# Casting the filter early on GpSimd, and making the swapped stage-P weights there too

## The chip, the cores and the metric

The kernel runs on one core of a Trainium2 chip. The metric is the device time of one execution in microseconds (us). Times are medians of several executions. All the runs used here are fast (a single core's runs are sorted only by how far they lie above the fastest of the same kernel), and the granted clock is named where it matters. Engines: TensorE (PE in the profile), VectorE (DVE), ScalarE (ACT), GpSimd (POOL), and SyncE (SP), which issues nearly all transfers.

## The reference

Eight sequences of 3008 x 256 are filtered in the frequency domain, then every token goes through a squared-ReLU feed-forward layer:

```python
X = np.fft.rfft(x, axis=1)                        # x: 8 x 3008 x 256, float32
Y = X * (filt_r + 1j * filt_i)[None, :, :]        # filters: 1505 x 256
y = np.fft.irfft(Y, n=3008, axis=1)
h = np.maximum(y.reshape(24064, 256) @ w_in, 0.0)   # w_in 256 x 2048
out = (h * h) @ w_out                               # w_out 2048 x 256
```

## The kernel before

The transform is split into stages. Stage A multiplies x by a small DFT matrix and writes u to memory (dU). u is read back transposed, stage B transforms it, VectorE multiplies by the filter F (the "products"), stage P transforms back, ScalarE evicts that as ze, and ze goes to memory (dZ). The z reads bring it back, and stage Y finishes y. Batch 0 goes through all this in a prologue. Batches 1 to 7 are woven into the feed-forward "stream", which takes over at the end of the prologue.

F has to be brought into the layout of stage B: the filter is cast to half precision (`f16`), then permutation matmuls "place" it into PSUM, from which it is evicted into `sF`. Stage P needs its weights twice for batch 0, once with the two halves of the partitions swapped (`sSPx`). The parts that matter here, with cuts marked:

```python
p_ze = tc.tile_pool(name="p_ze", bufs=3)    # ze: three groups of stage P in flight
p_h2 = tc.tile_pool(name="p_h2", bufs=2)    # two 16 KB buffers, used in turn
# ... third x tile of batch 0 (from p_h2), filters f32s[0], f32s[1] loaded on SyncE ...
u0 = p_h2.tile([96, NM, D], F16, tag="h2", name="u0")
for k, eng in enumerate((nc.vector, nc.vector, nc.gpsimd)):    # casts of batch 0's x
    ...
for c in (0, 2, 1, 3):
    chunk_a(0, c)            # stage A into u0
    write_u(0, c)            # u0 -> dU
# ... loads: half of sSB and sSP, u, the other halves, w_in, x(1,0), x(1,1) ...
f16s.append(p_h2.tile([128, 2, QF + D], F16, tag="h2", name="f16"))
for i in range(2):
    nc.gpsimd.tensor_copy(out=f16s[0][:, i, QF:], in_=nyq[:, i, :])
for im, eng in enumerate((nc.gpsimd, nc.vector)):
    for e in (slice(0, 1504), slice(1504, QF)):
        eng.tensor_copy(out=f16s[0][:, im, e], in_=f32s[im][:, e])
    for k in range(6):
        place_f(im, k)
for k, eng in enumerate((nc.vector, nc.gpsimd)):
    ...                      # sSPx, two copies of 64 x 1536 each
cast_win()                   # GpSimd
for c in range(2):
    cast_x(1, c, nc.gpsimd)
for r in range(14):
    if r < 12: unit_b(0, r)          # stage B and product
    if r >= 2: unit_p(0, r - 2)      # stage P, ze; a dZ write after every third
for c in range(4): read_z(0, c)
load_wout()
# ... x(1,2), x(1,3), stage A of batch 1, 12 warming matmuls, stage Y, stream ...
```

Of the kernel before, what the change touches and what calls it, by code (L numbers as in the profile page):

```python
# [9 lines left out]
F16 = mybir.dt.float16  # L10
# [9 lines left out]
QF = 3008  # L20
# [84 lines left out]
def kernel(  # L105
# [9 lines left out]
    nc = tc.nc  # L115
    B, S, D = x.shape
# [25 lines left out]
    p_h2 = ctx.enter_context(tc.tile_pool(name="p_h2", bufs=2))  # L142
# [63 lines left out]
    for k, v in enumerate((v0[:, 0:8, :], v1, v0[:, 8:16, :])):  # L206
        t = (p_h2 if k == 2 else p_x32).tile([128, 8, D], F32, tag="h2" if k == 2 else "x32",
                                             name=f"x0_{k}")
# [4 lines left out]
    f32s = []  # L213
# [10 lines left out]
    nyq = p_out.tile([128, 2, D], F32, tag="ost", name="nyq")  # L224
# [4 lines left out]
    sSP = const.tile([128, NC, 128], F16, name="sSP")  # L229
# [18 lines left out]
    f16s = []  # L248

    def place_f(im, k):  # L250

        banks, groups = bank_pair(f"psf_{im}_{k}")
        for i in range(4):
            c = 4 * k + i
            e0, e1 = D * c, D * (47 - c)
            cuts = [0] + [d for d in range(1, D)
                          if (e0 + d) % QF == 0 or (c and (e1 + d) % QF == 0)] + [D]
            for d0, d1 in zip(cuts, cuts[1:]):
                o = banks[i // 2][:, (i % 2) * D + d0:(i % 2) * D + d1]
                q, a = divmod(e0 + d0, QF)  # L260
                nc.tensor.matmul(o, sPF[:, PQ.index((0, q)), :], f16s[0][:, im, a:a + d1 - d0],  # L261
                                 start=True, stop=False)
                q, a = divmod(e1 + d0, QF) if c else (0, QF + d0)
                nc.tensor.matmul(o, sPF[:, PQ.index((1, q)), :], f16s[0][:, im, a:a + d1 - d0],  # L264
                                 start=False, stop=True)
        eng = pair_engine()
        for t, i in groups:
            n = t.shape[1]
            dst = sF[:, im, 4 * k + 2 * i:4 * k + 2 * i + 2 * n, :]
            src = t.rearrange("p t (a d) -> p (t a) d", d=D)  # L270
            if eng is nc.scalar:
                eng.activation(out=dst, in_=src, func=AF.Copy, scale=sign[:, 0:1] if im else 1.0)
            elif im:
                eng.tensor_scalar_mul(out=dst, in0=src, scalar1=sign[:, 0:1])
            else:
                eng.tensor_copy(out=dst, in_=src)
# [30 lines left out]
    def write_u(b, c):  # L307
        nc.sync.dma_start(
            out=dU[b].rearrange("(m q) d -> q m d", q=96)[:, 8 * c:8 * c + 8, :],
            in_=us.pop((b, c)))  # L310
# [18 lines left out]
    def chunk_a(b, c):  # L329

        if b == 0:
            u = u0[:, 8 * c:8 * c + 8, :]
        else:
            u = p_u.tile([96, 8, D], F16, tag="u", name=f"u_{b}_{c}")
        us[(b, c)] = u
        for k in range(2):
            banks, groups = bank_pair(f"psA_{b}_{c}_{k}")
            for i in range(2):
                m = slice(4 * k + 2 * i, 4 * k + 2 * i + 2)
                o = banks[i][0:96]  # L340
                if b == 0:
                    nc.tensor.matmul(o, s0[:, c // 2, :], x016[2 * (c % 2)][:, m, :],
                                     start=True, stop=False)
                    nc.tensor.matmul(o, s0[0:120, 2 + c, :], x016[1][0:120, m, :],  # L344
                                     start=False, stop=True)
                else:
                    nc.tensor.matmul(o, sSA, x16s[(b, c)][:, m, :], start=True, stop=True)
            eng = pair_engine()
            for t, i in groups:
                n = t.shape[1]  # L350
                o = u[:, 4 * k + 2 * i:4 * k + 2 * i + 2 * n, :]
                pv = t[0:96].rearrange("p t (a d) -> p (t a) d", d=D)
                if eng is nc.scalar:
                    eng.copy(out=o, in_=pv)
                else:
                    eng.tensor_copy(out=o, in_=pv)
# [190 lines left out]
    for k, eng in enumerate((nc.vector, nc.vector, nc.gpsimd)):  # L547
        for i in range(2):
            m = slice(4 * i, 4 * i + 4)
            eng.tensor_copy(out=x016[k][:, m, :], in_=x0[k][:, m, :])  # L550
    for c in (0, 2, 1, 3):
        chunk_a(0, c)
        write_u(0, c)
# [11 lines left out]
    for c in range(2):  # L565
        load_x(1, c)

    f16s.append(p_h2.tile([128, 2, QF + D], F16, tag="h2", name="f16"))
    for i in range(2):
        nc.gpsimd.tensor_copy(out=f16s[0][:, i, QF:], in_=nyq[:, i, :])  # L570
    for im, eng in enumerate((nc.gpsimd, nc.vector)):
        for e in (slice(0, 1504), slice(1504, QF)):
            eng.tensor_copy(out=f16s[0][:, im, e], in_=f32s[im][:, e])  # L573
        for k in range(6):
            place_f(im, k)

    for k, eng in enumerate((nc.vector, nc.gpsimd)):
        t = p_u.tile([128, 12, 128], F16, tag="u", name=f"sSPx_{k}")
        c = slice(12 * k, 12 * k + 12)
        eng.tensor_copy(out=t[0:64], in_=sSP[64:128, c, :])  # L580
        eng.tensor_copy(out=t[64:128], in_=sSP[0:64, c, :])
        sSPx.append(t)
    cast_win()
    for c in range(2):
# [25 lines left out]
    for s in range((NG + 1) * SLOTS):  # L610
        g, k = divmod(s, SLOTS)
# [40 lines left out]
```

## Time and profile before

| | before |
|---|---|
| time, median of the first 3 runs | 831.58 us (831.0 to 832.36) |
| span of the profiled run | 831.7 us |
| TensorE busy | 788.6 us, 95% |
| VectorE, ScalarE, GpSimd busy | 67%, 66%, 5% |
| first product | 49.94 us |
| w_out issued | 71.47 us |

The share of busy time belongs to the stream. To read the prologue one needs the chain of waits in order of time: each line is a piece of work with its start, its duration and its line in the source, and the next line could start only when it was over. The prediction below shows that chain for the first 90 us. Whatever shortens it ahead of the w_out transfer moves the rest of the program by the same amount, as long as nothing else becomes the last to arrive.

### The profile page before, as it was taken

To read this page: it belongs to the slowest core of one execution; us is meant where nothing else is said; L and a number is where in the kernel's file an instruction comes from. 1 tells how busy PE (TensorE), PEld (TensorE's weight loads), DVE (VectorE), ACT (ScalarE), POOL (GpSimd) and SP (SyncE) were. 2 spreads that over 40 slices of the span, in tenths; PEclk is the share of its full clock that TensorE was granted. 3 is DMA by queue.
4 is the path that set the end of the run, shared out by engine and by line. 5 is a ranking of instruction groups with operands and counts; after the bars stand their busy time and mean duration, and the time that the engine had idled before them with its cause. 6 is when DMAs were issued, how large, how long until landed. Compare 5 with 4: busy or idle time off the path is not lost.

```text
span 831.7 us, 14317 instructions
## 1 busy us (share of the span) xinstructions
PE 788.6 (95%) x5950; PEld 550.8 (66%) x5950; DVE 560.0 (67%) x879; ACT 548.4 (66%) x701; POOL 38.2 (5%) x45
## 2 busy tenths in 40 slices
PE   6566899899999999999999999999999999999997
PEld 3444466566767676776667767776767776676666
DVE  5394688557975599557985599656985589543331
ACT  2234667576777677776777767776777677666663
POOL 1330044000000000000000000000000000000000
PEclk9789999999999999999999999999999999999999
DMA  9928546634681545534582545624564432511111
GB/s 358 338 65 230 137 134 176 161 91 139 156 210 46 171 121 151 136 83 133 140 197 70 151 140 134 159 78 152 138 171 94 105 131 64 133 39 39 39 39 51
DMA packets 89376, 110.24 MB, mean 133 GB/s; under 512 B 4584, under 2 KB 80104, under 8 KB 84712
## 3 DMA queue, kind: packets, MB, share of 16 engines
q1 hardware_dynamic: 88960, 108.94, 46.7%
q8 instruction: 46, 0.75, 0.4%
q10 hardware_dynamic: 288, 0.39, 0.2%
q14 instruction: 18, 0.15, 0.1%
q0 software_dynamic: 64, 0.00, 0.0%
HBM read 59.51 MB, written 49.81 MB: 131 GB/s over the span
## 4 chain that ended last, share of the span: by engine, by line
PE 87%; DMA 5%; DVE 4%; issue 2%; SPq 0%; POOL 0%; ACT 0%; DVEq 0%; POOLq 0%; ACTq 0%
PE psO L490 38%; PE psH L475 37%; PE psA L318 3%; DMA x<-in_x_dram 2%; PE psB L368 2%; PE psY L445 2%; PE psP L404 2%; DMA wout<-in_moe_w_out_dram 2%; DVE prod L371 2%; PE psf L264 1%; PE psf L261 1%; DMA dU<-u 1%; DVE h L483 1%; PE psA L344 1%; DMA ut<-dU 0%
## 5 line engine op out<-in xcount | busy, mean ns | idle before, releaser
L479 ACT ACTIVATE h<-psH 128x1024 f16<-128x1024 f32 x376 | 385.0, 1025 | 194.4 <-PE psH L475 193.0
L475 PE MATMUL psH<-yt,sWin 128*128 128x512 f16 (+7 forms) x1728 | 388.3, 352 | 1.4 <-ACT h L479 0.7
L490 PE MATMUL psO<-sWout,h 128*128 128x256 f16 x3008 | 389.5, 273 | 0.0
L490 PEld LDWEIGHTS <-h 128*128 128x128 f16 x3008 | 291.4, 98 | 77.3 <-issue 0.5
L483 DVE TENSOR_TENSOR h<-h 128x1024 f16<-128x1024 f16 x376 | 259.0, 697 | 110.6 <-ACT h L479 110.3
L475 PEld LDWEIGHTS <-sWin 128*128 128x128 f16 x1728 | 160.1, 98 | 102.9 <-issue 4.7
L371 DVE TENSOR_TENSOR prod<-psB,sF 128x1024 f16<-128x1024 f32 x96 | 116.0, 1218 | 4.2 <-PE psB L368 3.4
L406 ACT CAST ze<-psP 128x512 f16<-128x512 f32 x96 | 56.3, 586 | 32.9 <-PE psP L404 17.8
L454 DVE CAST yt<-psY 128x376 f16<-128x376 f32 x64 | 35.1, 549 | 58.0 <-PE psY L445 53.0
L325 DVE CAST u<-psA 96x512 f16<-96x512 f32 x52 | 35.7, 687 | 49.3 <-PE psA L318 49.3
L497 ACT COPY ost<-psO 128x512 f32<-128x512 f32 x94 | 55.4, 589 | 6.8 <-PE psO L490 6.1
L445 PEld LDWEIGHTS <-zt 112*128 112x128 f16 x512 | 35.8, 98 | 23.2 <-issue 9.0
L445 PE MATMUL psY<-sC,zt 112*128 112x94 f16 x512 | 42.3, 206 | 4.3 <-DVE yt L454 2.0
L368 PE MATMUL psB<-ut,sSB 128*128 128x256 f16 x192 | 37.1, 276 | 9.3 <-DVE prod L371 8.8
L318 PE MATMUL psA<-x,sC 94*96 94x512 f16 x104 | 40.2, 388 | 3.7 <-DVE x L304 3.7
L368 PEld LDWEIGHTS <-sSB 128*128 128x128 f16 x192 | 18.9, 99 | 32.3 <-issue 13.3
L386 DVE TENSOR_TENSOR yf<-prod,yf 128x512 f16<-128x512 f16 x84 | 35.5, 423 | 3.0 <-POOL yf L380 0.5
L452 ACT CAST yt<-psY 128x376 f16<-128x376 f32 x64 | 29.9, 467 | 10.2 <-issue 5.1
L304 DVE CAST x<-x 94x2048 f16<-94x2048 f32 x26 | 31.6, 1217 | 4.7 <-DMA x<-in_x_dram 4.7
L404 PE MATMUL psP<-yf,sSP 128*128 128x256 f16 x168 | 32.1, 273 | 0.0
L323 ACT CAST u<-psA 96x512 f16<-96x512 f32 x52 | 29.8, 572 | 3.1 <-PE psA L318 3.1
L261 PE MATMUL psf<-f,sPF 128*128 128x256 f16 (+3 forms) x54 | 13.6, 299 | 10.5 <-POOL f L573 8.3
(53 smaller groups left out, 237.1 us busy)
## 6 DMA issues: line engine op xcount, KB each, us to landing
out_dram<-ost SPq DMA_DIRECT2D x94, 256.0 KB, 3.8
x<-in_x_dram SPq DMA_DIRECT2D x24, 768.0 KB, 5.9
dU<-u SPq DMA_DIRECT2D x32, 384.0 KB, 3.5
dZ<-ze SPq DMA_DIRECT2D x32, 384.0 KB, 3.1
zt<-dZ SPq DMA_DIRECT2D x64, 192.0 KB, 4.5
ut<-dU SPq DMA_DIRECT2D x8, 1024.0 KB, 5.8
ut<-dU SPq DMA_DIRECT2D x8, 512.0 KB, 3.9
x<-in_x_dram SPq DMA_DIRECT2D x3, 1024.0 KB, 7.5
```

Of the source, the lines that this page charges most:

```text
L318: nc.tensor.matmul(ps[0:96, :], sSA, x16s[(b, c)][:, 2 * i:2 * i + 2, :], start=True, stop=True)
L325: nc.vector.tensor_copy(out=o, in_=pv)
L368: nc.tensor.matmul(ps[:, i * D:(i + 1) * D], sSB[:, 2 * p + i, :], uts[b][:, 2 * p + i, :], start=True, stop=True)
L371: nc.vector.tensor_mul(out=prod, in0=ps.rearrange("p (a d) -> p a d", d=D).unsqueeze(1).to_broadcast([128, 2, 2, D]), in1=sF[:, :, 2 * p:2 ...
L404: nc.tensor.matmul(ps[:, i * D:(i + 1) * D], sSP[:, c2, :], prod[:, i, :], start=True, stop=True)
L406: nc.scalar.copy(out=zes[(b, c)][:, 2 * i6:2 * i6 + 2, :], in_=ps.rearrange("p (a d) -> p a d", d=D))
L445: nc.tensor.matmul(ps[:, 94 * jj:94 * jj + 94], zt[:, 4 * (g % 2) + jj, dt * 128:(dt + 1) * 128], sSY, start=True, stop=True)
L475: nc.tensor.matmul(ps[:, i, o:o + n], sWin[:, dt, jt * 128:(jt + 1) * 128], yts[b][:, dt, r:r + n], start=(dt == 0), stop=(dt == 1))
L479: nc.scalar.activation(out=h2[:, 2 * s:2 * s + 2, :], in_=ps, func=AF.Relu)
L483: nc.vector.tensor_mul(out=v, in0=v, in1=v)
L490: nc.tensor.matmul(pso[g][:, t % 2, :], h2s[g][:, jt, t * 128:(t + 1) * 128], sWout[:, jt, :], start=(jt == 0), stop=(jt == NJT - 1))
L497: nc.scalar.copy(out=ost, in_=pso[g])
```

## The change

The intent is to have F ready early. The casts of the filter move up in the program, ahead of stage A, and all of them go to GpSimd, which can run them as the filters land. In addition both swapped copies are made by GpSimd, so that VectorE can go from the last eviction of F straight to the products.

```diff
         for i in range(2):
             m = slice(4 * i, 4 * i + 4)
             eng.tensor_copy(out=x016[k][:, m, :], in_=x0[k][:, m, :])
+    f16s.append(p_h2.tile([128, 2, QF + D], F16, tag="h2", name="f16"))
+    for im in range(2):
+        nc.gpsimd.tensor_copy(out=f16s[0][:, im, QF:], in_=nyq[:, im, :])
+        for e in (slice(0, 1504), slice(1504, QF)):
+            nc.gpsimd.tensor_copy(out=f16s[0][:, im, e], in_=f32s[im][:, e])
     for c in (0, 2, 1, 3):
         chunk_a(0, c)
 ...
-    f16s.append(p_h2.tile([128, 2, QF + D], F16, tag="h2", name="f16"))
-    for i in range(2):
-        nc.gpsimd.tensor_copy(out=f16s[0][:, i, QF:], in_=nyq[:, i, :])
-    for im, eng in enumerate((nc.gpsimd, nc.vector)):
-        for e in (slice(0, 1504), slice(1504, QF)):
-            eng.tensor_copy(out=f16s[0][:, im, e], in_=f32s[im][:, e])
+    for im in range(2):
         for k in range(6):
             place_f(im, k)

-    for k, eng in enumerate((nc.vector, nc.gpsimd)):
+    for k in range(2):
         t = p_u.tile([128, 12, 128], F16, tag="u", name=f"sSPx_{k}")
         c = slice(12 * k, 12 * k + 12)
-        eng.tensor_copy(out=t[0:64], in_=sSP[64:128, c, :])
-        eng.tensor_copy(out=t[64:128], in_=sSP[0:64, c, :])
+        nc.gpsimd.tensor_copy(out=t[0:64], in_=sSP[64:128, c, :])
+        nc.gpsimd.tensor_copy(out=t[64:128], in_=sSP[0:64, c, :])
         sSPx.append(t)
```

## The prediction

> **What bounds the kernel now.** I read the page first. TensorE is busy 95% of the 831.7 us span, and from the fifth of the forty slices on all but the last stand at 8 or 9 tenths (the first four at 5 or 6). So the steady state, the feed-forward stream with the FFT of the next batch woven into it, is bound by TensorE, and the change touches none of its lines. Only the prologue is loose. There I followed the chain of waits in order of time, whole answer for the first 130 us. Columns: start, duration, what the end waited for.
>
> ```profile
> 18.61 1.30 DVE u L356 x2
> 19.96 4.91 DMA dU<-u
> 25.11 0.75 POOL f L570 x2
> 25.86 2.78 POOL f L573 x2
> ...
> 37.53 1.80 DVE f L573 x2
> ...
> 45.48 2.26 DVE sSPx L580
> 47.75 2.15 DVE sSPx L581
> 49.94 1.23 DVE prod L371
> ...
> 64.31 0.59 ACT ze L406
> 64.92 3.21 DMA dZ<-ze
> ...
> 71.47 14.34 DMA wout<-in_moe_w_out_dram
> 85.84 0.69 DVE sWout L296
> ```
>
> The chain waits for the write of dU (it empties the buffer u0, whose place f16 takes), then for the casts of F, first on GpSimd, then on VectorE, then for the two swapped copies on VectorE. Then come twelve products, the last dZ write, the z reads, w_out, and the stream. What starts before w_out is issued moves everything after it one for one. The list of waits names the first wait:
>
> ```profile
> POOL f L570 <- DMA dU<-u: 10.6, 1, 10.6
> ```
>
> Then I read GpSimd's and SyncE's instructions in order of time. GpSimd is free from 14.5 us, and the x loads of batch 1 stand in the queue early:
>
> ```profile
> 12.49 2.02 POOL L550 CAST x<-x 128x1024 f16<-128x1024 f32 x2 [9.82 <-DMA x<-in_x_dram]
> 27.65 0.96 SPq L186 DMA_DIRECT2D x<-in_x_dram  x2
> ```
>
> Last, the stretches (the last three numbers: granted clock, DMA share, GB/s):
>
> ```profile
> 23.80:27.20 3.40, 0.00 (x0) 0.00 (x0) 0.00 (x0) 0.00 (x0) 2.09 (x4) 0.50 0.79 262
> 37.80:41.20 3.40, 2.33 (x20) 1.95 (x21) 2.17 (x3) 1.27 (x2) 0.00 (x0) 1.00 1.03 224
> 41.20:44.60 3.40, 3.40 (x39) 3.12 (x38) 2.59 (x4) 2.38 (x3) 3.11 (x4) 1.00 0.76 183
> 44.60:48.00 3.40, 0.29 (x3) 0.11 (x2) 3.37 (x4) 0.00 (x0) 3.40 (x3) 0.95 0.05 14
> ```
>
> The queue is busy with w_in and the two x loads until about 46 us (the trace's last 8 KB packet of them ends at 46.06) and then empty. In the old kernel the first dZ write is issued at 55.6 us, into an empty queue. That will not be so any more.
>
> **What the skill says.** The Trainium skill, "TensorE: Matmul & The Clock Gate", section "What's actually happening": the clock falls to half after an idle window of 3.4 us and returns after a busy one. The trace agrees: TensorE idles from 19 to 27.3 us and the clock is 0.50 from 23.8 to 34.0. "DMA: Bandwidth & Descriptors", section "Two DMAs through the same engine are not ordered": in one queue of one DMA engine, descriptors start in order. The trace agrees: the first dU write is issued at 15.12 us, but its 512-byte packets begin at 18.11, as the 12,032-byte packets of the filters run out (the last ends at 19.12). "SBUF — State Buffer", section "SBUF: two separate sides": GpSimd and a VectorE operation in a two-port mode lock each other out. The trace fits: VectorE's 64x1536 copies took 2.26 and 2.15 us beside GpSimd's casts, GpSimd's own copies of that shape only 1.47 us. The products read one operand from PSUM, and ran at 1.21 us beside GpSimd's swaps after 113 us against 1.23 alone, so I charge them nothing.
>
> **The change, part by part.** The h2 pool has two buffers, given in turn. Before: third x tile, u0, w_in, f16. After: third x tile, u0, f16, w_in. So f16 waits only for GpSimd's own cast of that x tile (done 12.49 + 2.02 = 14.5), and w_in for the dU write, which SyncE already waits for ahead of it (it reads u at 25.0 us and issues w_in at 26.8). No new wait there.
>
> *Casts of F.* The real filter landed at 2.13 + 13.9 = 16.0 us; the imaginary one's last packet ended at 19.12, so it landed near 19.7. GpSimd: first small cast to 14.9, two halves at 1.42 us each (2.83 for both) from 16.0 to 18.9, small cast to 19.3, two halves from 19.7 to 22.6. VectorE loses 1.8 us of casts, GpSimd gains 2.8, off the path.
>
> *Placing F.* TensorE leaves stage A at 19.0 us. The imaginary half's placement ran at full clock from 38.52 to 44.30, with 0.35 of wait inside: 5.4 us. Two of them, with no cold stretch since there is no idle window: 19.0 + 10.8 = 29.8. The last eviction came 1.2 us after TensorE's end (44.24 to 45.47), so F stands at about 31.1 us, against 45.5. Of these 14.4 us, 8.3 are the idle before, 3.5 the cold first half (27.3 to 36.2 is 8.9 for 5.4), 2.3 the wait for VectorE's casts.
>
> *Swapped copies.* The 4.4 us on VectorE leave the path. GpSimd makes the first as soon as the first half of sSP is there (its last packet ends at 26.97): about 27.6 to 30.5. The second waits for the second half, as before: 34.39 to 37.3. The sixth pair of stage P, the first that needs it, comes after 38 us. Neither is late.
>
> *Products.* The first part of u is in at 25.0 + 4.7 = 29.7, so they start at 31.2 instead of 49.94: 18.7 us earlier. Twelve took 13.66 us (VectorE in order of time), so they end at 44.9.
>
> *What gives some back.* The ze pool has three buffers, so the fourth group of three pairs needs the first dZ write landed. That write came 5.64 us after the first product (55.58 - 49.94), so now at 36.9, when w_in and two x loads stand ahead of it in the same queue until 46.06. dU's 3072 packets passed in 6.4 us, often over 600 in a us; 768 packets of one dZ write then take some 1.2 us, and with 0.7 us to land it is in at about 48.0 (estimate). The tenth eviction of ze, which otherwise came at 31.2 + 11.2 = 42.4 (61.11 - 49.94 = 11.2), is held to 48.0. Tenth, eleventh, a stage-P pair, twelfth: 2.0 us. Then the dZ write 3.2 us and the z reads until the first stage-Y product 3.3 us (68.13 to 71.42): 48.0 + 2.0 + 3.2 + 3.3 = 56.5, against 71.42. **Sum: 14.9 us earlier**, 3.7 less than the 18.7 of the products.
>
> The casts of x on GpSimd stay where they were, since w_in lands at 41.4 as before: they end at 49.5 at the latest. Stage A of batch 1 follows the last stage-P product (49.3), needs them, and with its evictions and the warming matmuls (2.75 us warm, 5.1 cold) is over by 54.8 to 57: about even with the z reads. From w_out on all is as it was: issued at 56.5, landed 14.3 later.
>
> **Rivals.** (1) *The dZ writes are not held up*, because packets of several transfers pass each other: then the whole 18.7 us count and the time is 812.9. For it: the dZ write is small. Against: dU's packets waited for the filters', and for the later x loads too (at 88 us). (2) *GpSimd becomes the bound of F*, its casts 1.44 against 0.93 us on VectorE: TensorE would need the imaginary half at 24.4, which is ready at 22.6; even with F 5 us late, the products' tenth would come at 47.4, just within the 48.0. So this costs nothing until it is large; at 8 us late some 3 us come back: 819.6. (3) *The gain is hidden altogether* because the stream waits for w_in or its cast: w_in is cast by 45.5 us and the stream began at 79.2, so no. (4) *The warming stretch is cold*: TensorE idles from 44 to 48.5 behind the held ze, may lose its clock, and the warming matmuls end at 57 rather than 55: up to 0.7 us, 817.3. The stream's own phase against the 3.4 us clock windows adds about 1 us either way (two half-clock windows of 3.4 us stand in it now).
>
> **Range and chances.** 831.6 - 14.9 = 816.7. The range runs from rival 1 (812.9) to rival 2 (819.6), little widened. Two per cent is 814.95, a gain of 16.6 us; it needs the first dZ write landed before 46.3, which is hardly possible behind x, or rival 1. I give faster 0.25, within 0.74, slower 0.01.
>
> **What would show it.** Right: GpSimd's F casts from 16 to 22.6; the first placing matmul at 19.0 with no wait and no 0.50 clock before 44; the first product at 31, the twelfth over at 45; a wait of ScalarE's ze for DMA dZ of some 5 us near 43 to 48; w_out issued near 56.5 and landing 14.3 later; the stream's groups unchanged. Wrong: no such wait and w_out issued near 53 (rival 1); products after 36 (rival 2); or a w_out that is issued early but takes longer.

## The result

The changed kernel took 818.01 us (median of 4 runs, 816.32 to 819.82) beside 831.97 us for the kernel before (4 runs). The ratio is 0.9834, 95% interval 0.9805 to 0.9864. Ratios here are the mean time of one kernel's fast runs over the mean of the other's of the same rounds, so they are not quite the ratio of the medians. Later the same kernel took 817.12 us (6 runs, 814.47 to 819.97), ratio 0.9817. So the gain is 14 to 16 us, or 1.7 to 1.8%. The prediction was 816.7 us.

The chain of waits of the changed kernel, in order of time, from F's last eviction on (start, duration, what the end waited for):

```profile
30.33 0.90 DVE sF L274 x2
31.37 0.29 issue
31.65 1.72 DVE prod L371 x2
...
36.04 0.59 ACT ze L406
36.65 11.77 DMA dZ<-ze
48.51 0.59 ACT ze L406
49.15 1.03 PE psP L401 x4
50.20 0.59 ACT ze L406
50.81 3.19 DMA dZ<-ze
54.08 0.32 SPq L422
54.45 0.41 SPq L422
...
57.30 14.30 DMA wout<-in_moe_w_out_dram
```

The first product starts at 31.65 us, 18.3 us earlier than before. But w_out is issued only 14.2 us earlier (57.30 against 71.47). The 4 us between the two are lost in the second block. The chain leaves the products at 36 us and passes through a dZ write that takes 11.77 us from issue to landing, while the last one takes 3.19. After that last write SyncE issues the eight z reads (L422), one every 0.46 us, and only then, 3.3 us after the landing, w_out, which stands behind them in its program. The list of waits says who sat and waited for it:

```profile
ACT ze L406 <- DMA dZ<-ze: 5.1, 1, 5.1
```

GpSimd's instructions in order of time show the casts of F where they were meant to be, each filter cast as soon as it landed. (The bracket is the idle time before, and what ended it.)

```profile
16.06 2.83 POOL L555 CAST f<-f 128x1504 f16<-128x1504 f32 x2 [1.26 <-DMA f<-in_filt_r_dram]
19.69 2.82 POOL L555 CAST f<-f 128x1504 f16<-128x1504 f32 x2 [0.46 <-DMA f<-in_filt_i_dram]
```

VectorE's in order of time show something not foreseen, its first eviction of stage A after 3.27 us of idle time that GpSimd's cast of x ended:

```profile
14.49 1.22 DVE L356 CAST u<-psA 96x1024 f16<-96x1024 f32 x1 [3.27 <-POOL x L550]
```

The stretches of the changed kernel (busy time of TensorE, its weight loads, VectorE, ScalarE and GpSimd, then granted clock, DMA share and GB/s):

```profile
41.20:44.60 3.40, 2.45 (x21) 1.63 (x18) 3.40 (x4) 1.17 (x2) 1.75 (x2) 1.00 0.98 229
44.60:48.00 3.40, 0.25 (x3) 0.10 (x1) 0.71 (x1) 0.00 (x0) 3.40 (x4) 0.82 1.07 328
```

From 44.6 to 48 us TensorE, VectorE and ScalarE do next to nothing, while the transfers run at full share. In the kernel before the queue was empty in the same stretch (0.05). The stream itself has not changed: its two big matmul groups are busy 388.3 and 389.3 us, against 388.3 and 389.5 before.

### The profile page after: what moved, and what is told of

Read it like the earlier page. It is cut to its first block, busy times and chain, and to the rows that moved or that the text cites. A ratio compares the mean times of both kernels' runs of the same rounds, so it can differ in the third digit from the quotient of the medians.

```text
span 818.0 us, 14316 instructions
## 1 busy us (share of the span) xinstructions
PE 787.9 (96%) x5950; PEld 550.1 (67%) x5950; DVE 553.8 (68%) x875; ACT 548.3 (67%) x701; POOL 43.6 (5%) x49
## 4 chain that ended last, share of the span: by engine, by line
PE 87%; DMA 6%; DVE 3%; issue 2%; SPq 0%; ACT 0%; ACTq 0%; DVEq 0%
PE psO L490 38%; PE psH L475 37%; PE psA L318 3%; DMA x<-in_x_dram 2%; PE psY L445 2%; PE psB L368 2%; PE psP L404 2%; DMA dZ<-ze 2%; DMA wout<-in_moe_w_out_dram 2%; DVE prod L371 1%; PE psf L261 1%; PE psA L344 1%; PE psf L264 1%; PE psA L342 1%; DVE h L483 1%
## 5 line engine op out<-in xcount | busy, mean ns | idle before, releaser
L475 PE MATMUL psH<-yt,sWin 128*128 128x512 f16 (+7 forms) x1728 | 388.3, 352 | 1.4 <-ACT h L479 0.7
L490 PE MATMUL psO<-sWout,h 128*128 128x256 f16 x3008 | 389.3, 273 | 0.0
L325 DVE CAST u<-psA 96x512 f16<-96x512 f32 x52 | 35.7, 686 | 49.2 <-PE psA L318 49.2
L368 PEld LDWEIGHTS <-sSB 128*128 128x128 f16 x192 | 18.7, 98 | 29.1 <-issue 10.4
L323 ACT CAST u<-psA 96x512 f16<-96x512 f32 x52 | 29.8, 572 | 2.7 <-PE psA L318 2.7
L379 DVE COPY yf<-prod 64x512 f16<-64x512 f16 x72 | 20.8, 290 | 2.5
```

The costliest lines, as they stand in the source:

```text
L325: nc.vector.tensor_copy(out=o, in_=pv)
L368: nc.tensor.matmul(ps[:, i * D:(i + 1) * D], sSB[:, 2 * p + i, :], uts[b][:, 2 * p + i, :], start=True, stop=True)
L475: nc.tensor.matmul(ps[:, i, o:o + n], sWin[:, dt, jt * 128:(jt + 1) * 128], yts[b][:, dt, r:r + n], start=(dt == 0), stop=(dt == 1))
L490: nc.tensor.matmul(pso[g][:, t % 2, :], h2s[g][:, jt, t * 128:(t + 1) * 128], sWout[:, jt, :], start=(jt == 0), stop=(jt == NJT - 1))
```

## The experiments

Theory Q: the early products are held back by the transfers. The first dZ write stands behind w_in and the x loads of batch 1, the fourth group of ze waits for the buffer of the first, and so part of F's lead is given back. The rival views were that the products' own chain is the bound, that the small write is slow by itself, and that GpSimd's waits matter. Twelve kernels ran, and all gave the right result.

### F alone (e1)

The casts of F as in the change. The swapped copies stay split between VectorE and GpSimd as before:

```diff
-    for k in range(2):
+    for k, eng in enumerate((nc.vector, nc.gpsimd)):
-        nc.gpsimd.tensor_copy(...)
+        eng.tensor_copy(...)
```

> Change's F part alone; the swapped copies are split between VectorE and GpSimd as in the kernel before. Theory Q (the first dZ write waits in the queue behind w_in and x, and the fourth ze tile waits for it): products start 4.4 us later than in the changed kernel, at about 36, so the tenth ze would be ready near 47.2, still before the first dZ write lands (48.4, or later as it is now issued at about 41); w_out is issued within 1 us of the changed kernel's 57.3 and the time is 817 to 819: the swapped copies are worth nothing on top. Rival (products' chain is the bound, no queue effect): the two parts add, and this run is 4.4 us slower than the changed kernel, about 822.4.

Measured: 818.1 us (5 runs, 816.26 to 820.47), ratio 0.9833: the whole gain of the change. The swapped copies add nothing to the time that can be told from the scatter, as theory Q said. But the products did not start 4.4 us later, only 1.4 (33.03 against 31.65). The groups by line show why, first in the kernel before, then here:

```profile
L580 DVE COPY sSPx<-sSP 64x1536 f16<-64x1536 f16 x1 | 2.3, 2260 | 0.0
```

```profile
L580 DVE COPY sSPx<-sSP 64x1536 f16<-64x1536 f16 x1 | 0.6, 555 | 0.0
```

The same copy takes VectorE 2260 ns beside GpSimd's casts of x, and 555 ns when GpSimd waits at that time. In the kernel before, GpSimd's two casts end at 47.33 and 49.49 us, and VectorE's two copies beside them 0.41 us after each, at 47.74 and 49.91: a copy got through only when the cast was over. So it had been slow because of its neighbour. Once F is early, both copies together cost 1.1 us, not 4.4. In e1's profile ScalarE's wait for the first dZ write was 2.0 us instead of 5.1, partly because the products came later, partly because the write landed earlier (46.70). The chain then went through stage Y at half clock and not through w_out, so this profile alone doesn't show that the write set the end.

### The swapped copies alone (e2)

The kernel before, with only the second part of the diff.

> Only the swapped copies go to GpSimd; F is cast as before. Theory Q: products start at 45.5 instead of 49.9, the first dZ write is issued near 51 after the queue is empty (46), so nothing is given back: the whole 4.4 us count, about 827.5. Products start on a TensorE that did not idle, which changes nothing. Rival (the queue or w_in holds the end anyway): 831.5, no gain.

Measured: 829.14 us (6 runs, 826.4 to 830.8), ratio 0.9963 (0.9944 to 0.9982), a gain of 3 us where 4.4 was expected (the interval is a gain of 1.5 to 4.7 us, so 4.4 is not excluded). In its profile the first product starts at 47.19 us, 2.75 earlier than before. VectorE is through with F's evictions 1.7 us later (its next instruction starts at 47.19, against 45.48 before), and the clock stood at 0.50 for one more window (40.4 to 43.9) while the imaginary half was placed. Just before that window VectorE stood 0.2 us behind the kernel before (an eviction at 40.79 against 40.55), after it 1.8 (44.55 against 42.75), so the window accounts for nearly all of the delay. Part by part: F alone gains 14, the copies alone 3, both together 14.

### The dZ writes on ScalarE's queue (e3)

```diff
         if i6 == 2:
-            nc.sync.dma_start(
+            (nc.scalar if b == 0 else nc.sync).dma_start(
```

> Changed kernel, but batch 0's four dZ writes are issued from ScalarE's queue instead of SyncE's. Theory Q: the first dZ write lands within about 5 us of its issue at 36.7, the tenth ze runs at 42.8 without a wait, the last dZ write is issued near 46.4 and lands near 50, w_out is issued about 4 us earlier (53.3): about 814. Rival W (the write itself is slow while x loads use the engines and memory): landing still near 48, no gain, 818.

Measured: 817.34 us (5 runs, 813.05 to 819.1), ratio 0.9817 (0.9793 to 0.9842), not to be told from the changed kernel. ScalarE's instructions in order of time (DMA issues included):

```profile
37.72 0.38 ACTq L409 DMA_DIRECT2D dZ<-ze  x1
...
49.23 1.07 ACT L406 CAST ze<-psP 128x512 f16<-128x512 f32 x2 [5.53 <-DMA dZ<-ze]
```

Issued at 37.7 on a queue of its own, the write let ze go on only at 49.2. Its first 512-byte packet moved at 43.8, and most of them from 45 on, when the 8 KB packets of x had thinned out (29 in each us until 45, then 11). So theory Q's picture of one queue was wrong in this point: another queue did not help. That the engines which move the data were still taken up with x is the likely reason; what held the packets back on a queue of their own is not shown. Whether x holds the engines or the write is slow by itself is not told apart by this run. e8 below tells it.

### A fourth ze buffer (e4)

```diff
-            zes[(b, c)] = p_ze.tile([128, 6, D], F16, tag="ze", ...)
+            last = (b, c) == (0, 3)
+            zes[(b, c)] = (p_y if last else p_ze).tile([128, 6, D], F16, tag="yt" if last else "ze", ...)
```

> Changed kernel, but the fourth ze tile of batch 0 lies in a free filter buffer, so no ze eviction waits for a dZ write. Theory Q: the ze wait of 5 us is gone, the last dZ write is issued near 46.4, but stands behind x and the other three writes in the same queue and lands near 51, so w_out is issued near 54.3: about 815, 3 us better than the changed kernel. If only the buffer mattered and the queue did not: landing near 49.6 and about 813.5. If neither: 818.

Measured: 815.14 us (5 runs, 814.47 to 817.45), ratio 0.9806. As expected ze never waits for a write, the last dZ write is issued 4 us earlier, and it gives half of that back by standing behind the other transfers (5.01 us instead of 3.19). The chain of waits:

```profile
46.84 5.01 DMA dZ<-ze
55.14 14.51 DMA wout<-in_moe_w_out_dram
```

### u0 written first (e6)

In the change u0 lies in the buffer of the third x tile, because f16 is written first and takes the empty one. (This is read from the waits: the first evictions into u0 wait for GpSimd's cast of that x tile, and in this run they don't.) Here the casts of F stand after the first chunk of stage A:

```diff
     for c in (0, 2, 1, 3):
         chunk_a(0, c)
         write_u(0, c)
+        if c == 0:
+            ...    # f16 tile and its casts, moved here from ahead of the loop
```

> Changed kernel, but the casts of F stand after stage A's first chunk in the program, so that u0 is written first and gets the empty h2 buffer, and f16 gets the one of the third x tile. Theory: stage A's first evictions start at about 12.2 us instead of 14.5 (they no longer wait for GpSimd's cast of x), stage A ends about 1 us earlier, products start up to 1 us earlier; but the first dZ write still lands only after x, so the time stays with the changed kernel's, 817 to 819. Rival (the wait for GpSimd's cast is on the path): about 1.2 us faster, 816.5.

Measured: 815.49 us (6 runs, 812.44 to 818.78), ratio 0.9796 (0.9772 to 0.9819). ScalarE's evictions do start at 12.28 us, without the wait. But the first product came at 31.53, only 0.1 us earlier. What decides the end of stage A is not the wait but the clock, as the profiles of several kernels show together:

| profile | evictions wait for GpSimd's cast | half clock in stage A | stage A ends | first product |
|---|---|---|---|---|
| changed kernel | yes | 9.25 to 16.08 | 20.22 | 31.65 |
| e8 (below) | yes | 10.26 to 13.67 | 19.14 | 30.57 |
| e6 | no | 8.86 to 15.69 | 20.10 | 31.53 |
| e10 (below) | no | 10.69 to 14.10 | 19.04 | 30.48 |

One more half-clock window costs stage A some 1.1 us, the wait some 0.1. (e3 had one window too; its products waited for u instead.) The chain still ran through the first dZ write:

```profile
36.52 10.00 DMA dZ<-ze
```

It landed 1.9 us earlier than in the changed kernel's profile, as the last packet of x did (see the table below). Whether u0's place has a part in that is not shown: x's last packet ended between 44.38 and 45.49 us in the profiles of the five kernels that write u0 first and load x early (e6, e10 to e13), and between 45.19 and 47.85 in those of the five that write f16 first (changed kernel, e0, e1, e3, e4). The time is nearer to the rival's 816.5 than to the 817 to 819 of the theory. But the intervals of the two kernels overlap, and they ran in different calls, so whether u0's place alone is worth anything stays open.

### x out of the way (e8)

```diff
     load_win()
-    for c in range(2):
-        load_x(1, c)
 ...
     for c in range(4):
         read_z(0, c)
+    for c in range(2):
+        load_x(1, c)              # and their casts; then w_out
     ...
+    # stage A of batch 1 after stage Y, then x(1,2) and x(1,3)
```

> Changed kernel with batch 1's first two x loads issued after the z reads, ahead of w_out, and with stage A of batch 1 after stage Y. Theory (the dZ writes wait for x's transfers on the DMA engines, whichever ring they are on): the first dZ write, issued near 36.7, lands near 41, right after w_in; no ze eviction waits for a dZ write; the last dZ write is issued near 46.4 and lands near 49.6. Rival W (a 512-byte write is slow by itself at this time, or memory holds it): it lands near 48 again. The time is not the test, since x now delays w_out: between 812 and 820.

Measured: the first dZ write is issued at 35.57 and its packets move from 37.7 to 39.9 us, right behind w_in. None of the four dZ writes takes more than 6.4 us to land. ScalarE in order of time, tenth eviction, and the chain:

```profile
42.92 0.59 ACT L406 CAST ze<-psP 128x512 f16<-128x512 f32 x1 [0.59 <-PE psP L401]
```

```profile
45.55 3.17 DMA dZ<-ze
```

The tenth eviction waits for its matmul, not for a write, and the last dZ write lands 5.3 us earlier than in the changed kernel (48.72 against 54.00). So x's transfers, not the write, were what held it. The time was 820.44 us (4 runs, 819.02 to 821.23), as x now came too late for stage A of batch 1 (the chain shows 12.01 us for it).

### Two other orders of the transfers, and the clock (e9, e11, e13)

e9 puts x(1,0) and x(1,1) after the z reads, as in e8, with w_out right after the first dZ write; it, too, has u0 first, the fourth ze buffer, and w_out cast on GpSimd. e11 keeps x where it was, takes u0 first and the fourth ze buffer, and issues w_out ahead of the z reads:

```diff
+    load_wout()                  # e11: w_out before the z reads, cast on GpSimd
     for c in range(4):
         read_z(0, c)
-    load_wout()
```

> A version meant to beat both: changed kernel, u0 written first, fourth ze tile in a free filter buffer, batch 1's first x loads after the z reads with stage A of batch 1 after stage Y, w_out issued right after the first dZ write (its buffer is free when F is placed) and cast on GpSimd before the stream. Theory: w_out then lands near 47 instead of 71.6 and the stream does not wait for it (about 5 us), the z reads start near 51.5, the stream starts near 65: about 812. If x(1,0) and x(1,1) come too late for stage A (62 and later) the stream starts near 68 and it is about 815.

> The same with w_out issued ahead of the z reads (its buffer is free) and cast on GpSimd. Its 2 MB of 1 KB packets moved at some 340 packets in a us, 6 us; the z reads wait behind it, so stage Y starts some 2 to 4 us later, but the stream's second part no longer waits for w_out and its VectorE casts (5 us). Theory: 811 to 814. If the z reads lose more than the stream gains: 816 to 818.

Both missed: 822.06 us (5 runs, 819.92 to 825.33) and 821.39 us (4 runs, 819.75 to 823.02). In e9 the x loads took 12.4 us and came last, and its stage Y was at half clock too. In e11 the z reads landed near 60 us, and TensorE, idle after its 12 warming matmuls, ran all of stage Y at half clock. e13 is e11 with `keep_warm(40)` in place of `keep_warm(12)`:

> The version with w_out ahead of the z reads, with 40 warming matmuls instead of 12, so that TensorE does not idle for a clock window while the z reads wait. Theory (its loss against the combo was half the late z reads, half a stage Y at half clock, 11 us instead of 7.4): stage Y's matmuls take 203 ns again instead of 283 and the time falls by 3 to 4 us from 821.4, to about 817.5. Rival (the clock is not the cause): 821.

The stage-Y matmuls of e11, then of e13 (min, median and maximum in ns, first and last start):

```profile
L447 PE MATMUL psY<-sC,zt x64: 236/283/287, 60.3 to 71.3; 112*128 112x94 f16 x64
```

```profile
L447 PE MATMUL psY<-sC,zt x64: 202/204/208, 59.4 to 66.6; 112*128 112x94 f16 x64
```

e13 took 814.84 us (6 runs, 813.97 to 819.04): 6.5 us less than e11 in the medians, 5.7 by the ratios to the kernel before (they ran in different calls), more than the 3 to 4 expected. Stage Y is 3.8 us shorter and starts 0.9 earlier. The rest was not traced.

### The changed kernel again, and the versions that beat it (e0, e10, e12)

e0 is the changed kernel once more. e10 joins e4 and e6, and e12 is e10 with 18 warming matmuls instead of 12.

> The changed kernel unchanged, for its own scatter and as partner of the next two. Theory: the first dZ write lands 1.4 to 1.5 us after the last 8 KB packet of the x loads (46.91 to 48.42 in its profile), whose end moves from run to run (45.0 to 47.9 in four profiles so far), so its times scatter over some 3 to 4 us around 818.

> u0 written first and the fourth ze tile in a free filter buffer, together. The ze wait is gone as in the run with four ze tiles; the earlier products do not help, since the last dZ write still stands behind x and the other dZ writes. Theory: within 1 us of the run with the ze tile alone, 814.5 to 815.5, some 3 us under the changed kernel of this call. Rival (starting stage A's evictions earlier is worth its 1 us): 813.5 to 814.

> The best version so far (u0 first, fourth ze tile in a free filter buffer) with 18 warming matmuls ahead of stage Y instead of 12. Theory: stage Y is only sometimes at half clock there, so the median stays within 1.5 us of 813.2 and the slow outlier (817.5) may vanish. If the six more matmuls run cold they delay stage Y by up to 2.6 us less the idle it had: 815.

| kernel | median us | runs, range | ratio to before | 95% interval |
|---|---|---|---|---|
| e0, the change again | 817.12 | 6, 814.47 to 819.97 | 0.9817 | 0.9794 to 0.9839 |
| e10 | 813.20 | 6, 812.38 to 817.52 | 0.9787 | 0.9759 to 0.9815 |
| e12 | 812.55 | 5, 810.72 to 815.85 | 0.9769 | 0.9748 to 0.9791 |

e10 ran in the same call as e0 and beats it by 3.9 us in the medians. e12 is the fastest of all, though e10 and e12 are not told apart. e10 came out 1.3 us under the lower end expected from theory, and closer to the rival's 813.5 to 814, by which the early start of stage A is worth its 1 us. With e6 that is the second run in which the rival came closer. But in e10's profile the first product started early, at 30.48, because stage A had one half-clock window, not two, and the x loads also ended early (44.38). So the gain over e4 is not traced to u0.

The scatter of these kernels is 2 to 6 us; the kernel before also went from 829.25 to 833.37, 4 us. Two things change from profile to profile and may be behind it; that they make up the scatter was not tested. The first is the end of the x loads. The last 8 KB packet in the trace, and the moment when the first dZ write let ze go on:

| profile | last 8 KB packet ends | first dZ write landed | difference |
|---|---|---|---|
| e6 | 45.03 | 46.52 | 1.49 |
| e1 | 45.19 | 46.70 | 1.51 |
| changed kernel | 46.91 | 48.42 | 1.51 |
| e0 | 47.81 | 49.31 | 1.50 |
| e3 (own queue) | 47.85 | about 49.2 | 1.4 |

The second is the clock. In e0's profile stage Y ran at half clock from 60.9 us on, and the chain went through it instead of w_out. In the changed kernel's it did not.

## Why the prediction was right

Point by point, with what the runs showed.

**The casts and F.** GpSimd's casts of F ran from 16.06 to 22.51 us (predicted 16.0 to 22.6). Placing took 20.06 to about 30.6 at full clock with no wait (predicted 19.0 to 29.8). VectorE was through with F's evictions when the first product started at 31.65 (31.1 for F, 31.2 for the product), and the products ended at 45.31 (44.9). Rival 2, GpSimd as the bound of F, did not happen.

**What gives some back.** This step decided the size of the gain, and it held. The first dZ write was issued at 36.65 (36.9) and landed at 48.42 (48.0). ScalarE waited 5.1 us (some 5). w_out was issued at 57.30 (56.5) and took 14.30 us (14.3). e8 shows the cause by taking x away, e4 by taking the buffer away, and the table shows the landing following x's last packet in five profiles. That the size came out within 0.4 us is partly luck: 48.0 rests on x's last packet at 46.06, as in the one profile, and in the five of the table it ended between 45.03 and 47.85. So a landing near 46.3, which the prediction called hardly possible, was not far off (46.52 and 46.70 in e6 and e1). The mechanism was drawn too narrowly, as a queue: e3 shows that the write waits on another queue just as well. Rival 1, writes that pass the x loads, falls with it. It had been given the low end of the range.

**From the last dZ write to w_out.** The prediction took 3.3 us as the time from the write's landing to the first product of stage Y. The size was right (54.00 to 57.30), the path was not: w_out follows the issue of the eight z reads on SyncE, and the first product of stage Y started only at 58.1. In the kernel before the two stood together by chance (71.47 and 71.42).

**The swapped copies.** The prediction took their 4.4 us off the path in full and counted them in the 18.7 us of the products. Worked on the kernel before that is roughly so (3 us, e2). On top of an early F it is 1.1 us, and of the end time nothing that the scatter lets through (e1). The slowness of VectorE's copies came from GpSimd's casts beside them, and ScalarE had 5.1 us of wait to spare before the write's landing. The prediction had read the first of these facts off the trace (2.26 beside 1.47 us), but did not ask what VectorE's copy costs alone.

**The buffers.** Here a step failed. The prediction said that the buffers are given in the order in which the program asks for them, so that "f16 waits only for GpSimd's own cast of that x tile". In fact f16 took the empty buffer and u0 the one of the x tile, because f16 is written first. Stage A's evictions then waited for GpSimd until 14.49 us, instead of starting at 12.2. Stage A did end at 20.2 instead of 19.0, but by the table under e6 that was the clock: with the wait and one half-clock window it ended at 19.14 (e8), without the wait and with two windows at 20.10 (e6). What the wait costs the whole stays open (e6).

**The clock.** Predicted was no half clock before 44 us. There was one in stage A (9.25 to 16.08 us, against 10.14 to 13.55 before), and it is the 1.1 us by which stage A ended late; the first product was 0.5 us late in the end, as the placing took 10.5 us and not 10.8. Rival 4 came true in the profile: half clock from 46.8 to 57.0, warming matmuls of 4.24 us, stage Y starting at 58.2. It did not count there, as w_out was the last to arrive.

**Small slips.** The data of w_in was to land at 41.4 us as before; GpSimd got it at 42.85. In the prediction's own figures the first dZ write comes at 36.8 (31.2 + 5.64), not 36.9, the gain of 14.9 is 3.8 less than 18.7, not 3.7, and an F 8 us late would give back 2.4 us (50.4 against 48.0), not 3. None of these decides anything.

Of the remaining difference, 818.0 against 816.7, 0.8 us is on w_out's issue; the rest is within the scatter.

## What to carry to other kernels

When work is pulled forward, ask which transfers will then lie ahead of its own. A write that met an empty queue may now stand behind bulk loads that nobody needs yet, and its buffer holds up the engine. An instruction's duration in a trace includes its neighbours: before counting it as a gain, ask whether it would still be that long once the other part of the change is in. And two halves of a change are worth measuring singly: here one half carries all of the gain that can be told from the scatter.

## What the Trainium skill lacked or had wrong

- "DMA: Bandwidth & Descriptors", "Queues, rings and completion order", says that each DMA engine goes round between the queue rows it has work for, a packet at a time. In e3 a write issued at 37.7 us on ScalarE's row moved its first data at 43.8, and most of it from 45 on, as the loads on SyncE's row ran out, and landed no earlier than on SyncE's row (about 49.2 against 48.4). Why it did not get its turn earlier is open.
- No page gives the rate of the x loads of batch 1, 8 KB pieces for 96 partitions: 224 to 229 GB/s at a DMA share of 0.98 to 1.03 (the kernel before from 37.8 to 41.2 us, the changed kernel from 41.2 to 44.6), with some 28 packets in a us against 50 for w_in just before. Why is open.
- "SBUF — State Buffer", "SBUF: two separate sides", has the lock between GpSimd and VectorE without a size for such a copy: 64x1536 half-precision took VectorE 555 ns alone, and 2154 to 2260 ns beside GpSimd's casts of 94x2048.
